# The hand-over from attention to the expert layers: transposes behind the rank matmuls, low parts of late rows on VectorE, weights issued ahead of the row list

## The chip, the cores and the metric

The kernel runs on one core of a Trainium2 chip, in one launch. The metric is the device time of that core in microseconds; the number to forecast is the median of the runs of the changed kernel.

## The reference

Three layers follow each other. Masked attention over 4 batches, 8 heads, 576 positions and 64 dimensions (half of the heads local, half strided) gives 2304 rows of 512. Each row then goes to one of 8 experts, and the result goes through a squared-relu layer:

```
x = attn_out.transpose(0, 2, 1, 3).reshape(2304, 512)
e_idx = argmax(x @ w_gate, axis=1)
for e in range(8):
    mask = e_idx == e
    h = maximum(x[mask] @ w1[e], 0)          # 512 -> 1024
    out[mask] = gate_w[mask] * eom[mask, e] * (h @ w2[e])   # 1024 -> 512
y = maximum(out @ w_in, 0) ** 2 @ w_out      # 512 -> 2048 -> 512
```

## The kernel before

**Attention and routing.** Attention runs in units (a local pair of blocks or a strided residue of one batch), each in three steps: scores and softmax (`unit`), transpose of the probabilities (`unit2`), product with v (`unit3`). Its output lies transposed in `xT`. As soon as all units that a tile of 128 rows needs are done, `gates` makes the rows of that tile (`rw`, a matmul with an identity and the two gate matrices), copies them from PSUM to `xr`, and stores them to the table `x_d` in DRAM by SP's queue. There are 18 tiles in four groups; the last group is tiles 13 to 17, the "late" tiles (`LATE` is 13). `route` ranks the rows of a group within their expert (`rk` matmuls, then `posi`), and `scatter` writes each row's number to its place in the lists `tab_d` by an indirect DMA from POOL (GpSimd).

**The largest expert goes first.** After the third group `largest` finds the expert that has most rows so far (`e0`). `early_load` then has SP load that expert's row list (`ix`), has SP load the first two chunks of its first weight matrix (`r`, 512 KB each), and has POOL gather its rows out of `x_d` in four indirect DMAs (`win`). The matmuls of the late tiles don't go through DRAM: `late_rows` picks the wanted rows of the late tiles with 0/1 matrices `pm` that VectorE builds from the ranks, and adds them up in two PSUM tiles `lr`. For that the rows of a late tile are split into a high part `xa` (ScalarE) and a low part `xb` (POOL, by `LPOOL`). `first_rows` transposes the gathered rows (`wt`) or adds them to `lr` through an identity (`L596`). From `lr` come the last columns of `xh` and `xl`, and then the first expert matmul `h` runs.

**Weights.** Every weight chunk is split after its load into a high part `hw` (ScalarE, `prep_unit`) and a low part `lw` (VectorE). Three matmuls, hi by hi, hi by lo and lo by hi, stand for one (`mm3`).

**Order.** The program is written in one order and put in another by a scheduler with a cost model; `tc.issue_after(x)` keeps what stands in it behind instruction x on the same engine. Each engine runs its list in order, and SP's and POOL's DMAs are issued in list order. A tile name in a pool stands for a buffer in a ring: `xr` has four (`XRB`), so tile 17's rows take the buffer of tile 13.

Of the kernel before, what the change touches and what calls it, by code (L numbers as in the profile page):

```python
# [7 lines left out]
F32 = mybir.dt.float32  # L8
# [4 lines left out]
AF = mybir.ActivationFunctionType  # L13
ALU = mybir.AluOpType
# [5 lines left out]
B, H, S, HD = 4, 8, 576, 64  # L20
P = 128
NT = B * S
D = H * HD
KD = D // P
# [4 lines left out]
NTILE = NT // P  # L29
# [31 lines left out]
HB = 8  # L61

MG = [(3, 3), (3, 3), (3, 3)]
LPOOL = (13, 14, 15, 16, 17)
DS = 6
LN = 6
FILL = (2, 3)
PMB = 5
LWP = 0

# [61 lines left out]
def moe_kernel(ctx, tc, q, k, v, wg, wog, w1, w2, w_in64, w_out64, consts, out, dbg=None):  # L132
    nc = tc.nc
# [12 lines left out]
    ident = cst[:, C_ID : C_ID + P]  # L146
# [83 lines left out]
    for i in range(NPT):  # L230
        x = big.tile([P, 4, SM], F32, name=f"ptp{i}")
# [32 lines left out]
    last_ev, ev_ = {}, [None]  # L264
# [55 lines left out]
    nun = [0]  # L320
# [131 lines left out]
    scq = []  # L452
# [15 lines left out]
    def gates():  # L468
        while gq and needs(gq[0][1]) <= done:
            g, t = gq.pop(0)  # L470
            t0, t1 = GROUPS[g]
            if t == t0:
                xrs[g] = wk.tile([P, 5, 2 * E], F32, name=f"lg{g}", tag="lg", bufs=2), []
            lg, rows = xrs[g]
            xr = wk.tile([P, KD, W], F32, name=f"xr{t}", tag="xr", bufs=XRB)
            col = t * P % (2 * S)
            for kh in range(2):
                ps = pss.tile([P, 2, W], F32, name=f"rw{t}_{kh}", tag=TAILT.get((t, kh), "tp"))
                for kk in range(2):
                    kd = kh * 2 + kk  # L480
                    nc.tensor.matmul(ps[:, kk, :], xT[:, kd, col : col + P], igw[:, kd, :], start=True, stop=True)  # L481
                evac(xr[:, 2 * kh : 2 * kh + 2, :], ps)
            nc.vector.tensor_reduce(
                lg[:, t - t0, :], xr[:, :, P:].rearrange("p k c -> p c k"), axis=AX.X, op=ALU.add
            )
            rows.append(xr)
            if t >= LATE:
                parts[t] = xa, xb = [wk.tile([P, KD, P], F32R, name=f"x{i}{t}", tag="xp", bufs=XPB) for i in "ab"]
                nc.scalar.activation(xa, xr[:, :, :P], AF.Copy)
                eng = nc.gpsimd if t in LPOOL else nc.vector  # L490
                eng.tensor_tensor(xb, xr[:, :, :P], xa.bitcast(F32), op=ALU.subtract)
            stq(x_d[1 + t * P : 1 + (t + 1) * P, :], xr[:, :, :P])
            if t == t1 - 1:
                route(g, list(range(t0, t1)), lg, rows)
                if t1 == LATE:
                    lead["do"] = largest
                elif t0 >= LATE:
                    late_rows(t0, t1, rows)
# [6 lines left out]
    lead = {}  # L505
# [3 lines left out]
    oreg = {}  # L509
# [3 lines left out]
    def rows_of(k, reg):  # L513
        ix = const.tile([P, NW], I32, name=f"ix{k}")
        nw = (CAPS[k] + P - 1) // P
        nc.sync.dma_start(ix[:, :nw], tab_e[bass.ds(reg, 1), : nw * P].rearrange("e (c p) -> p (e c)", p=P))
        return ix
# [14 lines left out]
    def early_load():  # L532
        e0 = lead["e0"]
        oreg[0] = nc.values_load(e0[0:1, :], engines=[ET.SP], min_val=0, max_val=E - 1)
        lead["ix"] = rows_of(0, oreg[0])
        for c in range(2):
            raw = early[0].tile([P, KD, UC], F32, name=f"r0_{c}", tag="raw", bufs=2)
            nc.sync.dma_start(
                raw, w1[bass.ds(oreg[0], 1), :, c * UC : (c + 1) * UC].rearrange("e (a p) f -> p (e a) f", p=P)
            )  # L540
            eraw["w1", 0, c] = raw

        for r in range(0, CAPS[0], P):
            win_get(0, r, lead["ix"], 1 + LATE * P)
# [29 lines left out]
    def first_rows():  # L574

        xh = early[0].tile([P, KD, CAPS[0]], F32R, name="xh0", tag="xh")
        xl = early[0].tile([P, KD, CAPS[0]], F32R, name="xl0", tag="xl")
        xsp[0] = (xh, xl)
        acc["p"] = [pss.tile([P, 2, NL], F32, name=f"lr{h}", tag="pt") for h in range(2)]
        for t in range((CAPS[0] + P - 1) // P):  # L580
            R = min(P, CAPS[0] - t * P)
            w = wins[0, t]
            c = max(0, min(R, C0 - t * P))
            if c:
                ps = pss.tile([P, KD, P], F32, name=f"wt0_{t}", tag=("o", "os")[t % 2], bufs=1)
                for a in range(KD):
                    nc.tensor.transpose(ps[:, a, :c], w[:c, a, :], ident[:c, :c])
                cs = slice(t * P, t * P + c)
                nc.scalar.activation(xh[:, :, cs], ps[:, :, :c], AF.Copy)
                with tc.issue_after(lead["pm"].ins):  # L590
                    nc.vector.tensor_tensor(xl[:, :, cs], ps[:, :, :c], xh[:, :, cs].bitcast(F32), op=ALU.subtract)
            if c < R:
                cs = slice(t * P + c - C0, t * P + R - C0)
                with tc.issue_after(lead["rk"].ins) if t in FILL else nullcontext():
                    for a in range(KD):
                        nc.tensor.matmul(  # L596
                            acc["p"][a // 2][:, a % 2, cs],
                            w[:R, a, :],
                            ident[:R, c:R],
                            start=(t == C0 // P and a % 2 == 0),  # L600
                            stop=False,
                        )

    def late_rows(t0, t1, rows):
        rel = wk.tile([P, 5], F32, name=f"rel{t0}", tag="rel")
        nc.vector.tensor_scalar(rel[:, : t1 - t0], posi[:, t0:t1], lead["base"], None, op0=ALU.subtract)
        pms = []
        for t in range(t0, t1):
            pm = wk.tile([P, NL], F32R, name=f"pm{t}", tag="pm", bufs=PMB)
            lead["pm"] = nc.vector.tensor_scalar(  # L610
                pm, cst[:, C_IO : C_IO + NL], rel[:, t - t0 : t - t0 + 1], None, op0=ALU.is_equal
            )
            pms.append((t, pm))
        if t0 == LATE:
            first_rows()
        xh, xl = xsp[0]
        for h in range(2):
            ps = acc["p"][h]
            for t, pm in pms:
                for a in range(2):  # L620
                    for x in range(2):
                        nc.tensor.matmul(  # L622
                            ps[:, a, :],
                            parts[t][x][:, 2 * h + a, :],
                            pm,
                            start=False,
                            stop=(t == NTILE - 1 and a == x == 1),
                        )
            if t1 == NTILE:
                to = (slice(None), slice(2 * h, 2 * h + 2), slice(C0, CAPS[0]))  # L630
                nc.scalar.activation(xh[to], ps, AF.Copy)
                lead["last"] = nc.vector.tensor_tensor(xl[to], ps, xh[to].bitcast(F32), op=ALU.subtract)  # L632
# [94 lines left out]
    for b in range(B):  # L727
        t = tiles[b]
        tn = transposes(b + 1, tiles[b + 1]) if b + 1 < B else iter(())
        for n, ku in enumerate(ORDER[b].split()):  # L730
            next(tg, None)
            kind, u = ku[0], int(ku[1:])
            q2.append((b, t, kind, u) + unit(b, t, kind, u))
            drain(D2, D3)
            if b == B - 1 and n >= LN and "do" in lead:
                lead.pop("do")()
                lead["ok"] = 1
            if b == B - 1 and not early and all(a[0] == b for a in q2 + q3):
                front.close()
                early.append(  # L740
                    bulk.enter_context(tc.tile_pool(name="early", bufs=1, side="right", reuse_waits="tile"))
                )
            if scq and nun[0] >= scq[0][0] and (b < B - 1 or "ok" in lead):
                with tc.issue_after(last_ev["p"].ins):
                    scq.pop(0)[1]()
            if n >= (5 if b == 0 else 1):
                next(tn, None)
                if b == 0:
                    next(tn, None)
        for _ in tn:  # L750
            pass
        tg = iter(())
        if b + 2 < B:
            tiles[b + 2] = load(b + 2)
# [112 lines left out]
    def prep_unit(u):  # L867
        kind, k, c = u
# [42 lines left out]
        pool, nb = (raws, 2) if nwh[0] % WB < 2 else (mp, WB - 2)  # L911
        hi = pool.tile(shp, F32R, name="h" + nm, tag="wh", bufs=nb)
        first = u in eraw
        with tc.issue_after(last_ev["s"].ins) if first else nullcontext():
            nc.scalar.activation(hi, raw, AF.Copy)  # L915
        lo = pool.tile(shp, F32R, name="l" + nm, tag="wl", bufs=nb)
        eng = nc.gpsimd if first and LWP else nc.vector
# [472 lines left out]
```

## Time and profile before

| what | value |
|---|---|
| runs, us | 816.06, 822.29, 822.36 (median 822.29) |
| profiled execution, us | 815.72 |
| its span, us | 813.9 |
| busy TensorE (PE), us | 763.5 (94%) |
| busy VectorE, ScalarE, POOL, us | 553.9, 493.3, 216.8 |

The span is the stretch that the trace covers; 1.8 us of the profiled execution's own time lie outside it. Times in the trace count from the start of the span. Attention takes the first 150 us, the first expert matmul starts at 173.73 us, and the rest is expert layers and the last layer.

### The profile page before, as it was taken

The page shows a single profiled execution, that of the slowest core. Times are in us where ns is not written, and L with a number is a line of the kernel's source. Part 1 is how long each engine was busy: PE and PEld are TensorE (multiplying, and loading weights), DVE is VectorE, ACT ScalarE, POOL GpSimd, SP SyncE. Part 2 cuts the span into 40 slices and gives each one's busy share as a digit, 9 for nine tenths or more (in the row PEclk, how much of TensorE's full clock was granted, in tenths as well). Part 3 has the DMA queues.
Part 4 walks back from the last instruction along what each step waited for, and adds up shares of the span by engine and source line. Part 5 has one row for each costly group of instructions (what it writes and reads, how often), then busy time and mean ns, then how long its engine had stood idle before and what let it go on. Part 6 is the DMA issues. An engine that isn't in the chain of part 4 may idle for free.

```text
span 813.9 us, 14424 instructions
## 1 busy us (share of the span) xinstructions
PE 763.5 (94%) x5139; PEld 704.9 (87%) x5139; DVE 553.9 (68%) x1109; ACT 493.3 (61%) x1197; POOL 216.8 (27%) x210
## 2 busy tenths in 40 slices
PE   4999799599999999999989999999999999999993
PEld 3988789599999999999978888888889988888893
DVE  4778578565467578779889777787654687566442
ACT  2878588524455465656677676766655586556542
POOL 7223133537065764431133121004000003000002
PEclk9999989779999999999999999999999999999998
DMA  8987801629679999876554633524232235223002
GB/s 175 201 178 136 189 21 54 191 63 333 202 188 267 196 303 283 298 258 210 172 195 147 218 128 123 175 91 149 91 118 77 76 105 182 72 87 102 1 1 81
DMA packets 106691, 124.85 MB, mean 153 GB/s; under 512 B 42801, under 2 KB 77137, under 8 KB 106610
## 3 DMA queue, kind: packets, MB, share of 16 engines
q1 hardware_dynamic: 97026, 100.77, 43.6%
q0 software_dynamic: 8096, 22.63, 8.6%
q8 instruction: 42, 0.69, 0.4%
q10 hardware_dynamic: 1488, 0.44, 0.3%
q14 instruction: 39, 0.32, 0.2%
HBM read 101.70 MB, written 22.12 MB: 152 GB/s over the span
## 4 chain that ended last, share of the span: by engine, by line
PE 55%; issue 17%; DMA 9%; DVE 7%; ACT 6%; POOL 4%; SPq 1%; POOLq 0%; ACTq 0%; DVEq 0%
DMA s0wo<-in_moe_w_out_dram 4%; PE o L935 4%; PE h L935 4%; PE o L936 4%; PE o L937 4%; PE y L935 4%; PE y L936 3%; PE h L936 3%; PE y L937 3%; PE h L937 3%; PE rw L481 2%; DMA ks<-in_k_dram 1%; DMA rw<-in_moe_w_dram 1%; POOL win L520 1%; PE lr L622 1%
## 5 line engine op out<-in xcount | busy, mean ns | idle before, releaser
L935 PE MATMUL o<-hwo,gh 128*128 128x512 f32 x288 | 114.2, 397 | 3.8 <-ACT gh L1063 3.8
L936 PE MATMUL o<-lwo,gh 128*128 128x512 f32 x288 | 113.4, 394 | 0.0
L919 DVE TENSOR_TENSOR lw<-rw,hw 128x1024 fp32r<-128x1024 f32 x62 | 78.2, 1262 | 43.2 <-ACT hw L915 42.6
L1149 ACT ACTIVATE rl<-rl 128x384 f32<-128x384 f32 x96 | 49.5, 519 | 94.9 <-DVE rl L1147 94.8
L915 ACT ACTIVATE hw<-rw 128x1024 fp32r<-128x1024 f32 x62 | 65.9, 1062 | 65.2 <-PE h L936 44.9
L1176 POOL DMA_INDIRECT out_dram<-ob,idx x18 | 20.6, 1147 | 275.5 <-ACT ob L1175 271.0
L1064 DVE TENSOR_TENSOR gl<-rl,gh 128x384 fp32r<-128x384 f32 x96 | 56.8, 593 | 44.3 <-ACT gh L1063 43.2
L937 PE MATMUL o<-hwo,gl 128*128 128x512 f32 x288 | 83.6, 396 | 2.0 <-DVE gl L1064 2.0
L935 PE MATMUL h<-xh,hw 128*128 128x416 f32 (+7 forms) x256 | 81.0, 316 | 1.6 <-DVE hl L1035 1.5
L937 PE MATMUL h<-xh,lw 128*128 128x416 f32 (+7 forms) x256 | 79.5, 310 | 0.0
L936 PE MATMUL h<-xl,hw 128*128 128x416 f32 (+7 forms) x256 | 79.5, 310 | 0.0
L936 PE MATMUL y<-hl,hw 128*128 128x416 f32 (+7 forms) x256 | 77.1, 310 | 0.0
L937 PE MATMUL y<-hh,lw 128*128 128x416 f32 (+7 forms) x256 | 76.6, 310 | 0.0
L935 PE MATMUL y<-hh,hw 128*128 128x416 f32 (+7 forms) x256 | 68.0, 311 | 0.4 <-ACT hh L1034 0.4
L935 PEld LDWEIGHTS o<-hwo,gh 128*128 128x128 f32 x288 | 54.0, 188 | 15.5 <-ACT gh L1063 6.3
L937 PEld LDWEIGHTS o<-hwo,gl 128*128 128x128 f32 x288 | 53.6, 188 | 12.8 <-DVE gl L1064 3.0
L936 PEld LDWEIGHTS o<-lwo,gh 128*128 128x128 f32 x288 | 54.1, 188 | 9.0
L1063 ACT ACTIVATE gh<-rl 128x384 fp32r<-128x384 f32 x96 | 49.9, 521 | 1.8
L935 PEld LDWEIGHTS h<-xh,hw 128*128 128x128 f32 x256 | 48.1, 188 | 3.1 <-DVE hl L1035 2.9
L1150 ACT ACTIVATE rl<-rl 128x384 f32<-128x384 f32 x96 | 49.6, 519 | 1.7
L936 PEld LDWEIGHTS h<-xl,hw 128*128 128x128 f32 x256 | 48.2, 188 | 0.3 <-DVE xl L632 0.2
L936 PEld LDWEIGHTS y<-hl,hw 128*128 128x128 f32 x256 | 48.1, 188 | 0.1
(602 smaller groups left out, 2066.6 us busy)
## 6 DMA issues: line engine op xcount, KB each, us to landing
rw<-in_moe_w_dram SPq DMA_DIRECT2D x62, 512.0 KB
rwa<-ws_d SPq DMA_DIRECT2D x24, 512.0 KB
rwb<-ws_d SPq DMA_DIRECT2D x24, 384.0 KB
e6wi<-in_moe_w_in_dram SPq DMA_DIRECT2D x32, 256.0 KB
rwo<-wout_d SPq DMA_DIRECT2D x16, 512.0 KB
x_d<-xr SPq DMA_DIRECT2D x18, 256.0 KB
ws_d<-eo POOLq DMA_DIRECT2D x16, 256.0 KB, 5.1
s0wo<-in_moe_w_out_dram SPq DMA_DIRECT2D x8, 512.0 KB
```

What stands on the lines that cost most here:

```text
L481: nc.tensor.matmul(ps[:, kk, :], xT[:, kd, col : col + P], igw[:, kd, :], start=True, stop=True)
L520: return nc.gpsimd.indirect_dma_start(out=out_, out_offset=None, in_=x_d[:n, :], in_offset=bass.IndirectOffsetOnAxis(ap=ix, axis=0),)
L915: nc.scalar.activation(hi, raw, AF.Copy)
L919: eng.tensor_tensor(lo, raw, hi.bitcast(F32), op=ALU.subtract)
L935: nc.tensor.matmul(ps, ah, bh, start=first, stop=False)
L936: nc.tensor.matmul(ps, ah, bl_, start=False, stop=False)
L937: nc.tensor.matmul(ps, al, bh, start=False, stop=last)
L1063: nc.scalar.activation(h, x, AF.Copy)
L1064: nc.vector.tensor_tensor(l, x, h.bitcast(F32), op=ALU.subtract)
L1149: nc.scalar.activation(rl[:, :HC], src, AF.Relu)
L1150: nc.scalar.activation(rl[:, :HC], rl[:, :HC], AF.Square)
L1176: ins = nc.gpsimd.indirect_dma_start(out=out[:, :], out_offset=bass.IndirectOffsetOnAxis(ap=idx[:, gt_, 0:1], axis=0), in_=ob, in_offset=None,
```

## The change

Six edits, all in the last 35 us before the expert layers:

- `xb` of every late tile goes from POOL to VectorE; that of the last tile (17) is put behind the last `pm`.
- In `early_load` the two weight loads `r` are issued before the row list `ix`, not after it.
- All transposes and identity matmuls of gathered rows are put behind the rank matmuls `rk`, where only the third and fourth block were.
- The selection matmuls of `late_rows` run over all high parts first, then over all low parts, for each half.
- The high parts `hw` of the two early weight chunks are put behind the last `xa`; before, they stood behind the last ScalarE copy of the attention output.
- `largest` is called after the fourth unit of the last batch instead of the sixth, and up to two scatters are released per unit there.

```diff
-LPOOL = (13, 14, 15, 16, 17)
-LN = 6
-FILL = (2, 3)
+LN = 4
...
-                nc.scalar.activation(xa, xr[:, :, :P], AF.Copy)
-                eng = nc.gpsimd if t in LPOOL else nc.vector
-                eng.tensor_tensor(xb, xr[:, :, :P], xa.bitcast(F32), op=ALU.subtract)
+                lead["xa"] = nc.scalar.activation(xa, xr[:, :, :P], AF.Copy)
+                lead["xb"] = lambda: nc.vector.tensor_tensor(xb, xr[:, :, :P], xa.bitcast(F32), op=ALU.subtract)
+                if t < NTILE - 1:
+                    lead["xb"]()
...
-        lead["ix"] = rows_of(0, oreg[0])
         for c in range(2):
             raw = early[0].tile([P, KD, UC], F32, name=f"r0_{c}", tag="raw", bufs=2)
             nc.sync.dma_start(
...
             eraw["w1", 0, c] = raw
+        lead["ix"] = rows_of(0, oreg[0])
...
-                for a in range(KD):
-                    nc.tensor.transpose(ps[:, a, :c], w[:c, a, :], ident[:c, :c])
+                with tc.issue_after(lead["rk"].ins):
+                    for a in range(KD):
+                        nc.tensor.transpose(ps[:, a, :c], w[:c, a, :], ident[:c, :c])
...
-                with tc.issue_after(lead["rk"].ins) if t in FILL else nullcontext():
+                with tc.issue_after(lead["rk"].ins):
...
+        if t1 == NTILE:
+
+            with tc.issue_after(lead["pm"].ins):
+                lead["xb"]()
...
-            for t, pm in pms:
-                for a in range(2):
-                    for x in range(2):
+            for x in range(2):
+                for t, pm in pms:
+                    for a in range(2):
...
-                with tc.issue_after(last_ev["p"].ins):
-                    scq.pop(0)[1]()
+                for _ in range(2 if b == B - 1 else 1):
+                    if scq and nun[0] >= scq[0][0]:
+                        with tc.issue_after(last_ev["p"].ins):
+                            scq.pop(0)[1]()
...
-        with tc.issue_after(last_ev["s"].ins) if first else nullcontext():
+        with tc.issue_after(lead["xa"].ins) if first else nullcontext():
```

On SP, from the read of the largest expert's number (`e`) on, this stood in the program of before (`r` are the two weight chunks, `ix` the row list, `x_d<-xr` the stores of tiles 13 to 15):

```order
L516 DMA ix_2399<-tab_d 128x4x1
L538 ISA
L538 DMA r_0_2401<-in_moe_w_dram 128x4x256
L538 ISA
L538 DMA r_1_2403<-in_moe_w_dram 128x4x256
L501 DMA x_d<-xr_2471 512x1x128
L501 DMA x_d<-xr_2508 512x1x128
L501 DMA x_d<-xr_2533 512x1x128
```

and this stands at the same place in the change:

```order
L536 DMA r_0_2281<-in_moe_w_dram 128x4x256
L536 ISA
L536 DMA r_1_2283<-in_moe_w_dram 128x4x256
L500 DMA x_d<-xr_2471 512x1x128
L515 ISA
L515 DMA ix_2285<-tab_d 128x4x1
L500 DMA x_d<-xr_2508 512x1x128
L500 DMA x_d<-xr_2533 512x1x128
```

The weights and the store of tile 13 now stand ahead of the row list, which waits for the scatters.

On TensorE, from the last matmul of the late tiles' rows on, this stood in the program of before (`wt`, `lr` from `win` are the gathered rows, `rk` the ranks):

```order
L481 MATMUL rw_1_2584<-igw,xT 128x144 x2
L587 MATMUL wt_0_2636<-cst,win_0_2405 128x128 x4
L587 MATMUL wt_1_2643<-cst,win_128_2407 128x80 x4
L596 MATMUL lr_2634<-cst,win_128_2407 128x48 x2
L596 MATMUL lr_2635<-cst,win_128_2407 128x48 x2
L655 LDWEIGHTS cstb
L655 MATMUL rk_2605<-oh,cstb 128x40
```

and this stands there in the change (the twelve rows of `rk` between its first and its last are left out):

```order
L479 MATMUL rw_1_2584<-igw,xT 128x144 x2
L659 LDWEIGHTS cstb
L659 MATMUL rk_2604<-oh,cstb 128x40
...
L668 MATMUL rk_2604<-ebb,onesb 128x40
L587 MATMUL wt_0_2636<-cst,win_0_2287 128x128 x4
L587 MATMUL wt_1_2643<-cst,win_128_2289 128x80 x4
L596 MATMUL lr_2634<-cst,win_128_2289 128x48 x2
```

All ranks now stand ahead of everything that waits for a gather.

On ScalarE, from the last copy of the attention output (`xT`) on, this stood in the program of before (`xa`, `xr` are the high parts and the rows of tiles 15 to 17, `hw` the early weights' high parts):

```order
L274 ACTIVATE xT<-o3l_2573 128x2x64
L915 ACTIVATE hw_0_0_2775<-r_0_2401 128x1024
L915 ACTIVATE hw_0_1_2779<-r_1_2403 128x1024
L489 ACTIVATE xa_2543<-xr_2533 128x512
L274 ACTIVATE xr_2558<-rw_0_2559 128x288
L489 ACTIVATE xa_2568<-xr_2558 128x512
L274 ACTIVATE xr_2579<-rw_1_2584 128x288
```

and this stands there in the change:

```order
L272 ACTIVATE xT<-o3l_2573 128x2x64
L487 ACTIVATE xa_2543<-xr_2533 128x512
L272 ACTIVATE xr_2558<-rw_0_2559 128x288
L487 ACTIVATE xa_2568<-xr_2558 128x512
L272 ACTIVATE xr_2579<-rw_1_2584 128x288
L487 ACTIVATE xa_2589<-xr_2579 128x512
L921 ACTIVATE hw_0_0_2775<-r_0_2281 128x1024
```

The two `hw` moved behind the last tile's rows.

## Rows read from the trace of the kernel before

**Rows 1.** The page: busy us of each engine, share of the span, instructions.

```profile
PE 763.5 (94%) x5139; PEld 704.9 (87%) x5139; DVE 553.9 (68%) x1109; ACT 493.3 (61%) x1197; POOL 216.8 (27%) x210
```

**Rows 2.** TensorE's waits after 176 us: who waited for whom, us, times, longest.

```profile
PE o L935 <- ACT gh L1063: 3.8, 6, 0.8
```

**Rows 3.** TensorE, timeline: start us, us, what, count, [idle before <-releaser].

```profile
149.32 2.23 PE L481 MATMUL rw<-igw,xT 128*128 128x144 f32 x16 [0.53 <-DVE xT L270]
157.15 1.08 PE L587 MATMUL wt<-cst,win 128*128 128x128 f32 x4 [5.61 <-DMA win<-x_d,ix]
...
158.99 1.86 PE L596 MATMUL lr<-cst,win 128*128 128x48 f32 x8
163.10 0.22 PE L655 MATMUL rk<-oh,cstb 128*128 128x40 bf16 x1 [2.26 <-DVE oh L652]
...
163.53 3.92 PE L596 MATMUL lr<-cst,win 128*128 128x128 f32 x16
...
167.43 0.52 PE L622 MATMUL lr<-pm,xa 128*128 128x208 f32 x1
...
173.73 0.37 PE L935 MATMUL h<-xh,hw 128*128 128x416 f32 x1
```

**Rows 4.** Windows of 1 us: busy PE, PEld, DVE, ACT, POOL; PEclk, DMA share, GB/s.

```profile
151.00:152.00 1.00, 0.54 (x5) 0.33 (x3) 0.06 (x1) 0.00 (x0) 0.61 (x1) 1.00 1.00 282
...
154.00:155.00 1.00, 0.00 (x0) 0.00 (x0) 0.00 (x0) 0.56 (x2) 0.91 (x1) 0.54 1.21 350
...
161.00:162.00 1.00, 0.00 (x0) 0.00 (x0) 1.00 (x1) 0.00 (x0) 1.00 (x2) 0.50 0.92 314
...
171.00:172.00 1.00, 1.00 (x10) 1.00 (x10) 0.00 (x0) 0.00 (x0) 0.20 (x1) 0.92 0.02 1
```

**Rows 5.** VectorE, timeline: expert's number, late tiles' routing, early weights' low parts.

```profile
140.32 0.15 DVE L564 TENSOR_REDUCE e<-te 128x1 int32<-128x8 f32 x1
...
157.43 0.46 DVE L270 COPY xr<-rw 128x288 f32<-128x288 f32 x1 [6.37 <-POOL xb L491]
...
158.51 3.83 DVE L640 TENSOR_TENSOR d<-lg,mx 128x40 f32<-128x40 f32 x1
...
166.60 2.34 DVE L919 TENSOR_TENSOR lw<-r,hw 128x1024 fp32r<-128x1024 f32 x2
```

**Rows 6.** POOL, timeline: last early scatter, first gather, low parts, a late scatter.

```profile
141.95 1.23 POOL L703 DMA_INDIRECT tab_d<-tok,posi  x1 [0.30 <-issue]
151.39 0.99 POOL L520 DMA_INDIRECT win<-x_d,ix  x1 [8.21 <-issue]
...
156.11 6.17 POOL L491 TENSOR_TENSOR xb<-xr,xa 128x512 fp32r<-128x512 f32 x5
...
166.97 1.68 POOL L703 DMA_INDIRECT tab_d<-tok,posi  x1 [0.30 <-issue]
```

**Rows 7.** ScalarE, timeline: the first early weight split and the wait before it.

```profile
153.43 1.06 ACT L915 ACTIVATE hw<-r 128x1024 fp32r<-128x1024 f32 x1 [4.78 <-DMA r<-in_moe_w_dram]
```

**Rows 8.** SP's DMA queue, timeline: start us, us of issuing, what, count.

```profile
148.15 0.43 SPq L516 DMA_DIRECT2D ix<-tab_d  x1
148.82 0.97 SPq L538 DMA_DIRECT2D r<-in_moe_w_dram  x2
149.91 8.54 SPq L501 DMA_DIRECT2D x_d<-xr  x5
158.71 2.00 SPq L909 DMA_DIRECT2D rw<-in_moe_w_dram  x3
```

**Rows 9.** Tile `tab_d`, 141.8 to 143.3 us: its scatter.

```profile
DMA to landing us min/median/max: 6.2/6.2/6.2
```

**Rows 10.** Tile `tab_d`, 74.0 to 75.6 us: its scatter.

```profile
DMA to landing us min/median/max: 12.9/12.9/12.9
```

**Rows 11.** Tile `idx_d`, whole span: 18 scatters of the same kind.

```profile
DMA to landing us min/median/max: 6.9/7.5/9.5
```

**Rows 12.** Tile `win`, whole span: 24 gathers.

```profile
DMA to landing us min/median/max: 3.3/5.7/8.7
```

## The prediction

> **What bounds the kernel now.** I read the page first: TensorE is busy 763.5 us, 94% of the span [rows 1], so most of the span can only shrink by less TensorE work, and the change takes none away. The list of TensorE's waits then says where the rest is. After 176 us the largest group of waits adds up to 3.8 us [rows 2]; the expert layers follow TensorE, and whatever is won before them should move them forward as a block. So the whole question is how early the first expert matmul `h` starts; it starts at 173.73 us [rows 3].
>
> The timeline of TensorE shows three losses before it. The last rows matmuls end at 149.32 + 2.23 = 151.55 us; then TensorE stands idle for 5.61 us until the first gather has landed (157.15 us), and again for 2.26 us, up to 163.10 us, until VectorE has the one-hot matrix `oh` [rows 3]. Third, the clock: at 154 us it goes from its full level (2.4 GHz) to half of it (1.2 GHz), about 2.5 us after TensorE went idle, and it is back only in the slice from 171 us on [rows 4], so nearly all work between runs at half speed.
>
> The second loss has a chain of its own, in the other engines' timelines. ScalarE waits 4.78 us for the early weights and splits them from 153.43 us [rows 7], and the copies of the last tiles' rows stand behind that. POOL builds the low parts from 156.11 to 162.28 us [rows 6]. VectorE's copy of the last tile waits for one of them, since it takes the buffer of tile 13 (6.37 us), and its next two-input operation `d`, on 40 columns, takes 3.83 us and ends at 162.34 us, together with POOL's five [rows 5]. I take that as POOL holding VectorE up.
>
> The first loss is a chain of transfers. The last early scatter is issued at 141.95 us and lands after 6.2 us [rows 6, 9]; at 148.15 us SP issues the row list [rows 8]; at 151.39 us POOL issues the first gather [rows 6]; it is there at 157.15 us [rows 3], 5.8 us after its issue.
>
> **The change part by part.**
>
> *Low parts on VectorE, weight splits behind the late rows, ranks first.* These go together, since they all free the rank chain. On VectorE one `xb` has half the columns of an `lw`, which takes 2.34 / 2 = 1.17 us [rows 5], so about 0.6 us. Two stand ahead of the last copy into `xT`, for which the last rows matmuls wait; that delays them by 0 (VectorE has gaps there) to 1.2 us. From their end at 151.55 to 152.75 us it takes about 0.5 us for a copy, 1.1 us for what stands from the copy at 157.43 to the start of `d` at 158.51 us [rows 5], 0.2 us for an undisturbed `d`, 0.8 us from its end to the ranks [rows 3, 5], and 0.6 us for the `xb` of tile 16: 3.2 us. The ranks then run at 154.8 to 156.0 us instead of 163.10 us, in the idle time ahead of the gathered rows. What goes from TensorE's path is the wait of 2.26 us and the ranks themselves, 163.53 - 163.10 = 0.43 us: **-2.7 us**. The weights are no new wait on ScalarE: issued 6 to 7 us earlier, they are there before the last `xa`. `pm`, the last `xb` (0.6 us) and both `lw` (2.34 us) follow the ranks on VectorE and are done by about 161 us; the selection matmuls that need the first two start later than that. If that cover were gone, the last `xb` would cost 0.6 us.
>
> *Weights ahead of the row list on SP.* The two loads (1 MB) are issued as soon as SP has read the expert's number, which VectorE has ready at 140.5 us [rows 5], so while the last scatters go out (the last at 141.95 us [rows 6]); the store of tile 13 follows them, and its rows are copied by then, so the row list still comes to its wait before the scatters land. What this can cost is the landing of the scatters. The nearest rows on both sides: 6.2 us beside almost no traffic [rows 9], and a median of 7.5 us for the index scatters beside weight loads [rows 11]. So 0 to +1.3 us; I take half, **+0.7 us**, as the burst covers only part of the flight. The far bound is 12.9 us for a scatter beside many small transfers [rows 10]; it is a rival below.
>
> *What the gathers gain.* In the trace the gathers share the DMA engines with the weights and with stores of 256 KB each; the engines are full from 151 us on [rows 4]. With the weights gone the landing of the first, 5.8 us, should come nearer to the shortest of the tile, 3.3 us [rows 12]. Against that, the stores of tiles 16 and 17 and the next three weight chunks, which SP issues at 158.71 us [rows 8], move forward to about 153 us. I take 4.5 us, the middle: **-1.3 us**, with ends of -2.5 and 0.
>
> *Ranks ahead of gathered rows, order of the selection matmuls, earlier call of `largest`.* The number of matmuls stays. High parts first means that the last `xb` is wanted late and the first half is complete some 2 us earlier; both are covered by what stands beside, so 0. `largest` and the first scatter move, but the scatters of the third group wait for their ranks as before: 0.
>
> *The clock.* Gathered rows take 160.85 - 157.15 = 3.7 and 167.43 - 163.53 = 3.9 us, the forty selection matmuls 173.73 - 167.43 = 6.3 us [rows 3]. Of these 6.3 us about 3.65 run at half the clock, until it rises [rows 4]. If a matmul takes twice as long at half the clock, all forty take 9.0 us at 1.2 GHz and 4.5 us at 2.4 GHz (an estimate from these rows). The clock fell within an idle time, and the change leaves TensorE idle from about 152 to 156.5 us but for 0.4 us of ranks; I take it to fall again and to rise at the same place in the work, **0**, with ends of -1.8 and +2.7 us.
>
> The sum is -2.7 + 0.7 - 1.3 + 0 = -3.3 us: gathered rows from 156.55 us, selection from 164.15 us, `h` at 170.45 us. Against the profiled execution's 815.72 us this is 812.4 us.
>
> **Two rules.** Row first: beside `lw` (166.60 to 168.94 us) a scatter took 1.68 us on POOL where the undisturbed gather took 0.99 [rows 5, 6]. The Trainium skill ("SBUF — State Buffer", "Who interferes with whom") says that a VectorE operation with two SBUF inputs contends with POOL operations that read SBUF and that the second to come waits; it speaks against `xb` on VectorE while POOL issues gathers. By the row one gather beside an `xb` would come at most 0.7 us later, and the sum would be -2.6 us.
>
> The scatters' price is the more open one. The Trainium skill ("DMA: Bandwidth & Descriptors", "Queues, rings and completion order") says that a DMA engine takes turns between queues, packet by packet. Were that all, SP's megabyte would hold a POOL scatter up by little, and the sum would be -4.0 us. The 7.5 us beside weight loads [rows 11] agree only in part, so I keep +0.7.
>
> **The rivals.**
>
> *The scatters sink in the weights (slower).* If the last early scatter lands as late as the one beside heavy traffic, 12.9 instead of 6.2 us [rows 9, 10], the row list, the gathers and all behind them come 6.7 us later. With the other terms that is +6.7 - 1.3 - 2.7 = +2.7 us: 818.4 us. It decides from a delay of 4 us on, a landing of 10.2 us. For it: the two loads start exactly when the last scatters do. Against it: eighteen scatters beside weight streams stayed at or under 9.5 us [rows 11].
>
> *The next weights meet the gathers.* SP now issues 1.5 MB more some 5 us earlier, beside the later gathers. If the third, issued some 2.6 us after the first (four take 156.11 - 151.39 = 4.7 us [rows 6]), lands after the longest time, 8.7 us [rows 12], it is there at 163.4 us, and TensorE wants it at 156.55 + 3.7 = 160.3 us: a new wait of 3.1 us takes the place of the one removed. Time: 815.5 us.
>
> *The clock doesn't fall.* The ranks now break the idle time, which was about 2.5 us old when the clock fell. At full clock the gathered rows' 7.6 us halve, but the last gather, issued about 155.9 us, lands some 5 us later (between shortest and median [rows 12]), so selection starts at about 161.2 us and `h` at 165.7 us: -8.0 us, 807.7 us. Against it: two idle stretches of 1.5 us and more remain, and the ranks are a few small matmuls.
>
> **How the numbers follow.** The forecast has 0.63, with a range of its own of 809 to 815.5 us on the profile's scale; the sunken scatters 0.10, the colliding weights 0.15, the kept clock 0.12. The executions of the kernel before lie in two pairs, 815.72 and 816.06, 822.29 and 822.36 us; the trace is of the lower pair, and no row says what the other 6.5 us are. The forecast against the lower pair is 812.4 us, against the median of the runs 822.29 - 3.3 = 819.0 us. A median of the changed kernel can come out at either; I give the middle, 815.7 us, which is 0.4% from both. The range runs from the kept clock in the lower pair (807.5) to beyond the forecast in the upper one (821); it leaves out the sunken scatters in the upper pair and what else ends under 807.5.
>
> Faster or slower by 1% is about what a measurement of this kernel can tell from no change, as its own runs differ by 0.8%. One per cent is 8.2 us: the forecast reaches that only if its median falls in the lower pair and the other kernel's in the upper one; the kept clock just about reaches it alone. That gives 0.19 for faster. Slower by 1% needs the sunken scatters and an unlucky pair: 0.03. The rest, 0.78, lies within 1%.
>
> **What would show it.** In the profile of the changed kernel: the ranks at 154 to 156 us, ahead of the first transposed gathered row; `d` at 0.2 us; no wait of VectorE's copies for POOL; early weight splits without a wait for a DMA; the landing of the last early scatter under 7.6 us and of the first gather near 4.5 us; half clock from about 154 us until the selection matmuls are under way; `h` at about 170.5 us. The forecast is wrong if a gather makes TensorE wait after the first one, if the row list is issued later than 149.5 us, if the clock rises earlier or later by more than 2 us, or if waits after `h` grow by more than 1 us.

## The result, and the profile after

The changed kernel takes **824.0 us** (median of 20 runs, 820.85 to 829.35), the kernel before 819.35 us (20 runs beside them, 815.90 to 822.36). The ratio is **1.0065, 95% interval 1.0048 to 1.0081**: slower by 0.65%. The forecast was 815.7 us with a range of 807.5 to 821.0; the sign was wrong and the time lies above the range, though within the 1% that held most of the chances.

The profiled execution of the changed kernel took 824.17 us (span 822.3), against 815.72 us for the profile of before, which is one of the kernel's faster executions. The medians differ by less, 4.65 us. Of the 8.45 us, 2.0 lie ahead of the steps below (the last early scatter is issued at 143.93 instead of 141.95 us); 1.9 of them are there already when SP issues its stores at 128.77 instead of 126.83 us, ahead of the earlier call of `largest`. So each step below is counted from that scatter.

The page, answering to [rows 1] (busy us, share, instructions), and TensorE's waits after 182.5 us, answering to [rows 2]: neither shows where the time went.

```profile
PE 763.6 (93%) x5139; PEld 704.3 (86%) x5139; DVE 554.4 (67%) x1114; ACT 494.1 (60%) x1197; POOL 211.0 (26%) x205
```

```profile
PE o L941 <- ACT gh L1069: 4.1, 7, 0.9
```

TensorE's timeline, answering to [rows 3] (start us, us, what, count, idle before and its releaser), shows it:

```profile
151.40 2.23 PE L479 MATMUL rw<-igw,xT 128*128 128x144 f32 x16 [0.67 <-DVE xT L268]
161.61 0.21 PE L659 MATMUL rk<-oh,cstb 128*128 128x40 bf16 x1 [7.99 <-DVE oh L656]
...
167.04 1.12 PE L587 MATMUL wt<-cst,win 128*128 128x128 f32 x4 [4.93 <-DMA win<-x_d,ix]
169.75 0.79 PE L587 MATMUL wt<-cst,win 80*128 80x80 f32 x4 [1.60 <-DMA win<-x_d,ix]
170.34 5.54 PE L596 MATMUL lr<-cst,win 128*128 128x48 f32 x24
175.81 2.46 PE L626 MATMUL lr<-pm,xa 128*128 128x208 f32 x10
...
182.46 0.43 PE L941 MATMUL h<-xh,hw 128*128 128x416 f32 x1
```

The order is as intended: ranks `rk` ahead of the first transposed gathered row `wt`, and `lr` behind it in one piece. But TensorE is idle for 8.0 us ahead of the ranks (2.3 before) and for 4.9 us ahead of `wt` (5.6 before). The chain that ended last (start us, us, what) says on what:

```profile
143.93 14.40 DMA tab_d<-tok,posi
...
158.83 2.49 DMA x_d<-xr
...
162.60 7.11 DMA win<-x_d,ix
```

and the tile `tab_d`, 143.9 to 144.5 us, answers to [rows 9]:

```profile
DMA to landing us min/median/max: 14.4/14.4/14.4
```

The last early scatter lands after 14.4 us instead of 6.2. SP's DMA queue, answering to [rows 8], stands at its wait for it:

```profile
143.52 1.03 SPq L536 DMA_DIRECT2D r<-in_moe_w_dram  x2
146.51 0.55 SPq L500 DMA_DIRECT2D x_d<-xr  x1
158.35 0.37 SPq L515 DMA_DIRECT2D ix<-tab_d  x1
158.83 2.60 SPq L500 DMA_DIRECT2D x_d<-xr  x4
```

POOL, answering to [rows 6], issues the scatter 0.41 us behind the first weight load and the first gather only 3 us behind the row list:

```profile
143.93 1.19 POOL L707 DMA_INDIRECT tab_d<-tok,posi  x1 [0.30 <-issue]
161.31 0.99 POOL L519 DMA_INDIRECT win<-x_d,ix  x1 [16.18 <-DMA x_d<-xr]
...
165.13 1.76 POOL L519 DMA_INDIRECT win<-x_d,ix  x1 [0.30 <-issue]
```

VectorE, answering to [rows 5], has lost the hold by POOL (`d` takes 0.20 us instead of 3.83), and its copy of the last tile has a new wait in the old one's place, for a store:

```profile
159.00 0.46 DVE L268 COPY xr<-rw 128x288 f32<-128x288 f32 x1 [5.86 <-DMA x_d<-xr]
...
160.65 0.20 DVE L644 TENSOR_TENSOR d<-lg,mx 128x40 f32<-128x40 f32 x1
```

Windows of 1 us, answering to [rows 4] (busy PE, PEld, DVE, ACT, POOL; PEclk, DMA share, GB/s):

```profile
144.00:145.00 1.00, 1.00 (x9) 0.78 (x8) 1.00 (x3) 1.00 (x8) 1.00 (x1) 1.00 1.91 12
...
149.00:150.00 1.00, 1.00 (x14) 0.85 (x14) 0.97 (x3) 0.52 (x1) 0.00 (x0) 1.00 0.52 29
...
152.00:153.00 1.00, 1.00 (x11) 1.00 (x10) 0.32 (x1) 0.41 (x1) 0.00 (x0) 1.00 1.03 364
...
156.00:157.00 1.00, 0.00 (x0) 0.00 (x0) 0.00 (x0) 0.00 (x0) 0.00 (x0) 0.63 0.00 0
```

```profile
180.00:181.00 1.00, 1.00 (x10) 1.00 (x10) 0.06 (x1) 0.52 (x1) 0.00 (x0) 0.93 0.00 0
```

From 144 us on the DMA engines count as busy and move little; the megabyte goes by from 152 us on, and then nothing moves until the list is issued. (A share can exceed 1, since the whole time of a packet, one piece of a transfer, is booked where it starts: next to the 1.91 of 144 us stands 0.00 for 145 to 146 us.) The clock is at its lower level (1.2 GHz) from 156.3 us, in the idle time, to 180 us.

Counted from the last early scatter's issue to the first `h`, step by step (each a difference of two starts in the rows above, and of the same starts in [rows 3, 6, 8]):

| step | before, us | after, us | difference |
|---|---|---|---|
| last early scatter issued to row list issued | 6.20 | 14.42 | +8.2 |
| row list to first gather | 3.24 | 2.96 | -0.3 |
| first gather to `wt` | 5.76 | 5.73 | 0.0 |
| `wt` to first selection matmul | 10.28 | 8.77 | -1.5 |
| selection to `h` | 6.30 | 6.65 | +0.4 |
| sum | 31.78 | 38.53 | +6.75 |

With the 2.0 us ahead of it and 0.3 us less behind `h`, that is the 8.45 us between the two profiles. The same interval in each profile below is called **scatter to h**.

### The profile page after: what moved, and what is told of

Read it like the earlier page. It is cut to its first block, busy times and chain, and to the rows that moved or that the text cites. A ratio compares the mean times of both kernels' runs of the same rounds, so it can differ in the third digit from the quotient of the medians.

```text
span 822.3 us, 14426 instructions
## 1 busy us (share of the span) xinstructions
PE 763.6 (93%) x5139; PEld 704.3 (86%) x5139; DVE 554.4 (67%) x1114; ACT 494.1 (60%) x1197; POOL 211.0 (26%) x205
## 4 chain that ended last, share of the span: by engine, by line
PE 60%; issue 17%; DMA 9%; ACT 5%; DVE 3%; POOL 3%; SPq 1%; POOLq 0%; ACTq 0%; DVEq 0%
PE o L941 5%; PE o L943 5%; PE o L942 5%; PE h L941 4%; PE y L941 4%; PE y L942 4%; PE h L942 4%; PE h L943 4%; PE y L943 4%; DMA s0wo<-in_moe_w_out_dram 3%; DMA ks<-in_k_dram 2%; DMA tab_d<-tok,posi 2%; PE rw L479 1%; POOL idx_d L833 1%; DMA win<-x_d,ix 1%
```

## The experiments

**Theory A**: the loss is the meeting of the two weight loads (1 MB) with the scatters, whose landing releases the row list; the rest of the change gains. **Rival B**: the loss lies in the other parts (ranks ahead of the weight splits, low parts on VectorE, the buffer that tile 17 waits for), and the late landing is covered or accidental. **Rival C**: what delays the scatter is any traffic ahead of it, or the store of tile 13 alone. They were run in three sessions, each on another chip: experiments 2 to 5, with the first run of 3, in the first, experiments 1, 6 and 7 in the second, experiment 8 and the second run of 3 in the third. Each ratio is to the kernel before in the same session (medians there 821.02, 819.46 and 819.40 us).

**1. The change and the kernel before, again.** No edit; the first timed, of the second one profile.

> The change itself once more, unaltered, beside the other runs of this call. Theory A (the weight loads go out between the scatters and hold the last one up): 1.004 to 1.008 of the kernel before, landing of the last early scatter over 10 us. Rival F (its loss belonged to the one chip of the first measurement): within 0.2% of the kernel before.

> The kernel before once more, for a second profile of it: the first one was of an execution of 815.72 us, where most take 817 to 822. Expected: the same waits as in the first profile, with the rise of the clock later or a longer wait for transfers in the batches before, 3 to 5 us more in all.

Measured: the change 824.54 us, 1.0059 [1.0038, 1.0080]; before, one execution, 820.66 us. In the change the first load left at 143.99 us, again 0.41 us ahead of the last scatter, and that landed after 15.9 us; scatter to h 39.1 us. In the kernel before the scatter landed in 6.3 us and scatter to h was 33.3 us, 1.4 us more than in its first profile, all of it in the selection matmuls (178.87 - 171.17 = 7.7 us instead of 6.3), as the clock came back later. So two profiles of one kernel differ by that much in this interval; the 5.3 to 7.3 us by which the two of the change are longer are more.

**2. Row list first, the rest of the change kept.**

```diff
         oreg[0] = nc.values_load(e0[0:1, :], engines=[ET.SP], min_val=0, max_val=E - 1)
+        lead["ix"] = rows_of(0, oreg[0])
         for c in range(2):
...
             eraw["w1", 0, c] = raw
-        lead["ix"] = rows_of(0, oreg[0])
```

> The change with one part undone: the row list is issued ahead of the two weight loads again (the store of tile 13 then stands behind it too); all else of the change stays. Theory A (weight loads issued while the scatters are in flight hold the scatters up, and that is the whole loss): the last early scatter lands after 6 to 7 us instead of 14.4, the first matmul h starts 3 to 5 us earlier than in the kernel before, time 0.995 to 0.997 of it. Rival B (the moved low parts, ranks and weight splits cost something themselves): the landing is short again, but the time stays at or above 1.003 of the kernel before.

Measured: 818.29 us, **0.9968** [0.9946, 0.9989]. The list goes out 6.0 us behind the last scatter. With the one order undone the change is faster than the kernel before by 0.3%: against B, though the unaltered change was not timed beside it; experiment 7 was timed beside the change. That `h` would come 3 to 5 us earlier was missed: scatter to h is 34.3 us in this profile, with 5.0 us from the list to the first gather, and TensorE is at the last tiles' rows until 160.8 us.

**3. Only the weights ahead of the list, in the kernel before; twice.**

```diff
-        lead["ix"] = rows_of(0, oreg[0])
         for c in range(2):
...
             eraw["w1", 0, c] = raw
+        lead["ix"] = rows_of(0, oreg[0])
```

> The kernel before with one part of the change alone: the two weight loads (and with them the store of tile 13) stand ahead of the row list. Theory A: the last early scatter lands after 12 us or more, the first gather comes some 8 us later, the old waits for ranks fall inside that delay, time 1.005 to 1.009 of the kernel before. Rival B: within 0.2% of the kernel before, landing under 8 us.

> The kernel before with the two weight loads ahead of the row list, once more, to see on which side of the last early scatter the loads leave. If they leave ahead of it, as in the change, its landing takes 13 to 16 us and the time is 1.004 to 1.009 of before; if they leave behind it, the landing takes 6 to 8 us and the time is 0.999 to 1.003.

Measured: first 820.79 us, 1.0006 [0.9987, 1.0024]; in the third session, the same kernel, 824.16 us, **1.0040** [1.0008, 1.0071]. The first result missed what A expected. The two intervals overlap, so that the times differ is not certain; the profiles show what differed. First session, POOL's last early scatter and SP's queue:

```profile
141.40 0.97 POOL L703 DMA_INDIRECT tab_d<-tok,posi  x1 [0.30 <-issue]
```

```profile
143.31 0.54 SPq L537 DMA_DIRECT2D r<-in_moe_w_dram  x2
147.98 0.55 SPq L501 DMA_DIRECT2D x_d<-xr  x1
148.78 0.41 SPq L516 DMA_DIRECT2D ix<-tab_d  x1
```

Third session, the same two:

```profile
144.31 1.21 POOL L703 DMA_INDIRECT tab_d<-tok,posi  x1 [0.30 <-issue]
```

```profile
143.93 1.03 SPq L537 DMA_DIRECT2D r<-in_moe_w_dram  x2
146.92 0.55 SPq L501 DMA_DIRECT2D x_d<-xr  x1
160.52 0.37 SPq L516 DMA_DIRECT2D ix<-tab_d  x1
```

The program is the same. In the first the loads left 1.9 us behind the last scatter, and the list was issued 7.4 us after it (815.57 us, the fastest of the twelve runs); in the second they left 0.38 us ahead of it, and it landed after 16.2 us (824.44 us). Scatter to h was 31.2 us in the first and 35.5 us in the second. So A holds in a narrower form: in these profiles it counts on which side of the last scatter the loads leave. Other parts of the change aren't in this kernel, so they aren't needed for the loss.

What set the two apart lies ahead of the loads. In all four profiles of the first session ScalarE stands idle for 3.5 us ahead of a copy `ptp`, with a releaser that the profile doesn't show ("remote"); here for the first profile above:

```profile
ACT ptp L274 <- remote: 3.5, 1, 3.5
```

There VectorE starts on the expert's number 0.3 to 0.4 us ahead of the last scatter's issue; in every profile without this idle time it does so 1.6 to 1.7 us ahead. SP needs the number for the loads' addresses. Whether the chip or chance brings the idle time, no run tells. The other executions have no trace, so on which side their loads left isn't known.

**4. Other bytes ahead of the list.** The list first of the weights, but behind two stores of 256 KB each to a tensor that nothing reads.

```diff
+        for i in range(2):
+            nc.sync.dma_start(
+                spare_d[bass.ds(oreg[0], 1), i].rearrange("e p (k c) -> p (e k) c", c=P), igw[:, :, :P]
+            )
+        lead["ix"] = rows_of(0, oreg[0])
```

> The change, but with two stores of 256 KB from SBUF to a spare DRAM tensor in the place of the weight loads, and the weights behind the row list; 0.5 MB more is moved. Theory A as a matter of any transfer that SP starts beside the scatters: landing 10 us or more and a time of at least 1.003 of the kernel before. Rival C (only loads from DRAM do it): landing 6 to 8 us, time 0.995 to 0.999.

Measured: 818.89 us, 0.9988 [0.9968, 1.0009]. The stores left at 145.85 us, behind the last scatter (144.00 us), and SP needed 7.43 us to issue them, which by itself puts the list 9.5 us behind the scatter. So it doesn't tell loads from stores; inconclusive on C. Scatter to h was 34.2 us. Against experiment 2 a list that is 3.5 us later goes with 0.2% more time, within the intervals.

**5. One load ahead of the list, the other behind.**

```diff
             eraw["w1", 0, c] = raw
-        lead["ix"] = rows_of(0, oreg[0])
+            if c == 0:
+                lead["ix"] = rows_of(0, oreg[0])
```

> The change, but only one of the two weight chunks (512 KB) ahead of the row list; the second and the store of tile 13 behind it. If the cost goes with the bytes in flight: landing about 10 us, time about the kernel before's. If one load is enough to set it off: landing 13 us or more, time 1.004 to 1.008. Rival D (the store of tile 13, not the weights, holds the row list up): landing 6 to 7 us, time 0.995 to 0.998.

Measured: 820.22 us, 1.0003 [0.9976, 1.0029]. Here too the load left behind the last scatter (146.03 against 144.19 us), the list 6.8 us after it, and the first gather 6.2 us after the list instead of 3.2 [rows 6, 8]. Scatter to h was 34.8 us. It doesn't say whether one load ahead of the scatter is enough for the delay.

**6. Both loads ahead of the list, but behind the store of tile 13,** so that they can't leave ahead of the last scatter.

```diff
+            st = stq(x_d[1 + t * P : 1 + (t + 1) * P, :], xr[:, :, :P])
+            if t == LATE:
+                early_rest(st)
...
+        with tc.issue_after(st.ins):
+            early_weights()
+        lead["ix"] = rows_of(0, oreg[0])
```

> The change with one shift: the two weight loads still stand ahead of the row list, but behind the store of tile 13, and so go out some 2 us later, after the last early scatter has left POOL. Theory A2 (what counts is that the loads go out before the last scatter): landing 6 to 8 us, time 0.997 to 1.001 of the kernel before. Rival G (loads in flight at any time between scatter and row list cost the same, or the list queues behind them): landing or list some 6 us late as in the change, 1.004 to 1.008.

Measured: 820.36 us, **1.0005** [0.9985, 1.0026], in the session in which the unaltered change had 1.0059. POOL's last early scatter, and SP's queue:

```profile
145.81 1.19 POOL L715 DMA_INDIRECT tab_d<-tok,posi  x1 [0.30 <-issue]
159.51 0.99 POOL L521 DMA_INDIRECT win<-x_d,ix  x1 [12.52 <-DMA x_d<-xr]
```

```profile
149.18 2.64 SPq L548 DMA_DIRECT2D r<-in_moe_w_dram  x2
153.00 0.37 SPq L517 DMA_DIRECT2D ix<-tab_d  x1
```

The scatter lands in 7.1 us. What is left is a second, smaller loss: the list's own trip to the first gather takes 6.5 us instead of 3.2. So in these profiles the loads cost wherever they stand ahead of the list: 8 to 10 us for the scatter if they leave just ahead of it, about 1 us for the scatter and 3 us for the list if behind. Scatter to h was 34.2 us.

**7. List first, weights behind the last tile's store.**

```diff
         oreg[0] = nc.values_load(e0[0:1, :], engines=[ET.SP], min_val=0, max_val=E - 1)
+        lead["ix"] = rows_of(0, oreg[0])
...
+            if t == NTILE - 1:
+                with tc.issue_after(st.ins):
+                    early_weights()
```

> The change with the row list first and the two weight loads last, behind the store of the last tile. Theory: the gathers share the DMA engines only with stores, the first lands after about 4 us instead of 5.6, and the weights still arrive ahead of their use: 0.993 to 0.996 of the kernel before, 1 to 2 us under the run with the list first alone. Rival: the weights come late, ScalarE waits for them ahead of the transposed rows' high parts, and the time is that of the kernel before or above.

Measured: 817.55 us, **0.9979** [0.9958, 1.0000], less of a gain than expected, in the session in which the unaltered change had 1.0059. In its profile (816.65 us) scatter to h is the shortest of all, 30.8 us: the scatter lands in 6.1 us, the list needs 3.4, the first gather 4.8 us.

**8. The loads long before the last scatters.** The kernel leaves out the choice of the expert for the first two chunks: they are those of expert 0, so their loads need not wait for its number.

```diff
-                raw, w1[bass.ds(oreg[0], 1), :, c * UC : (c + 1) * UC].rearrange("e (a p) f -> p (e a) f", p=P)
+                raw, w1[0:1, :, c * UC : (c + 1) * UC].rearrange("e (a p) f -> p (e a) f", p=P)
```

> The first two chunks are loaded from expert 0 whatever the router says (the choice of the expert for them is left out), so that they can leave SyncE some twenty microseconds ahead of the scatters and have landed when the scatters go. If the loss of the change is the meeting of weight bytes and scatters, the last scatter lands after 6 to 7 us, the row list is issued at about 149 to 150 us, the first selection runs 30 to 32 us after the last scatter's issue and the time is 0.996 to 0.999 of before. If the loss came from the other parts of the change (ranks ahead of the weight splits, low parts on VectorE), it stays at 1.004 to 1.007.

Measured: 816.66 us, **0.9966** [0.9936, 0.9997]. SP's queue, POOL, TensorE:

```profile
114.94 0.94 SPq L536 DMA_DIRECT2D r<-in_moe_w_dram  x2
...
150.25 0.42 SPq L515 DMA_DIRECT2D ix<-tab_d  x1
```

```profile
143.95 1.19 POOL L707 DMA_INDIRECT tab_d<-tok,posi  x1 [0.30 <-issue]
153.59 0.99 POOL L519 DMA_INDIRECT win<-x_d,ix  x1 [8.45 <-DMA x_d<-xr]
```

```profile
156.16 0.19 PE L659 MATMUL rk<-oh,cstb 128*128 128x40 bf16 x1 [2.52 <-DVE oh L656]
159.57 1.11 PE L587 MATMUL wt<-cst,win 128*128 128x128 f32 x4 [2.97 <-DMA win<-x_d,ix]
...
168.41 2.46 PE L626 MATMUL lr<-pm,xa 128*128 128x208 f32 x10
```

The store of tile 13 is issued behind the list here; all else stands as in the change. The scatter lands in 6.3 us and the loss is gone: A over B. Scatter to h is 31.8 us; it is this interval that came out at the 30 to 32 us expected for the first selection matmul, which starts after 24.5 us. As for C, the store can't be the sole cause, since the engines crawl from 144 us on and it is issued at 146.51 us, later than an undelayed scatter's packets run (below); whether it adds to it was not tried. Of the versions that compute all, experiment 2 beats the kernel before; experiment 7 beats the change in one session, and the kernel before by an interval that ends at 1.0000.

## Why the prediction was wrong

**The step that failed** is "Weights ahead of the row list on SP", put at +0.7 us. It measured +8.2 us in the change's first profile and 9.7 in its second (15.9 - 6.2). The step saw the place (the loads leave while the last scatters go out) but took its price from [rows 11], index scatters beside weight loads that stream already, at 7.5 us, and kept 12.9 us [rows 10] only for a rival. That was the near row, and "many small transfers" misread it. In the kernel before, a load of 576 KB (`qs`) left 1.2 us ahead of that scatter and another (`ks`) 0.4 us behind it, SP's queue and POOL:

```profile
73.39 0.31 SPq L244 DMA_DIRECT2D qs<-in_q_dram  x1
74.92 0.31 SPq L244 DMA_DIRECT2D ks<-in_k_dram  x1
```

```profile
74.56 1.00 POOL L703 DMA_INDIRECT tab_d<-tok,posi  x1 [0.17 <-issue]
```

So the meeting stood in the trace before, at a price of 6.7 us (12.9 - 6.2). Experiment 8 shows that the price belongs to what is sent at this place, and experiments 1, 3 and 6 that it hangs on which leaves first: with the loads 0.38 to 0.41 us ahead of the last scatter it lands after 14.4, 15.9 and 16.2 us, with loads 1.8 to 3.4 us behind it the list goes out after 6.8 to 7.4 us (experiments 3, 5 and 6). What lies between these two was not seen. The prediction compared durations of landing and didn't ask which of two engines' queues would be first.

**The slower rival** had the mechanism, "The scatters sink in the weights", and its point of decision, a landing of 10.2 us. Its price was too low, 6.7 us against 8.2 to 9.7, and the gains of 4.0 us that it set against that were 1.4 in the table. Its chance of 0.10 rested on the eighteen scatters of [rows 11] and not on the one of [rows 10], which was nearer.

The Trainium skill ("DMA: Bandwidth & Descriptors", "Queues, rings and completion order") has a DMA engine take turns between queues, packet by packet. The prediction took from it that the scatter would be held up by little; the landings of 14.4 to 16.2 us show that here more was at work.

**A wait that was not seen**: the store of tile 13 is issued behind the loads at 146.51 us and crawls with them, so the copy of tile 17, which takes its buffer in the ring of four, waits for it until 159.00 us, and the ranks stand at 161.61 us instead of the 154 to 156 forecast. The gathers, held by the list, came later still (`wt` at 167.04 us), so it probably cost little of its own here; in experiment 8, where the store isn't behind the loads, the ranks run at 156.16 us. Its price alone was not tried.

**The ranks, low parts and weight splits, -2.7 us**: the mechanism was right, the size was not. `d` takes 0.20 us, no copy waits for POOL, the ranks are out of the gathered rows' way, the early splits don't wait for a DMA. From `wt` to the selection the change saves 1.5 us, experiment 8 1.4 us (8.84 us), experiment 7 0.6 us (9.67 us, with 2.96 us of wait for the second gather inside). The rest went into a second gather that TensorE now waits for (1.60 us in the change): shorter work in front uncovers it. The gather itself, -1.3 us, gave 0.0 in the change, -1.0 in experiment 7 and +0.2 in experiment 8.

**The clock, 0**: it fell in the idle time as forecast and rose 4.3 us into the selection matmuls instead of 3.7 (by the share of the lower level in the window at either rise): selection to h takes 6.65 us in the change, 6.9 in experiment 7 and 7.3 in experiment 8, up to 1.0 us given back. As the kernel before had 7.7 us in its second profile, this term is no property of the change. Behind `h` nothing changed, as forecast (waits for `gh` 4.1 us against 3.8).

Taken together, the change without its loads ahead of the list is worth 0.21% to 0.34% (experiments 7, 2 and 8; the last with expert 0's chunks), that is 1.7 to 2.8 us of 819.4; the prediction's sum without that step was -4.0 us. The scale was no part of the miss: with the 20 runs' median the same sum gives 819.35 - 3.3 = 816.05 us, close to the middle of two scales that was given.

**How the scatter was held up** can be read from the DMA queues (packets, MB, share of 16 engines): q0 has POOL's scatters, 32 packets each, q1 SP's transfers, q8 and q14 instructions. In the changed kernel the three scatters ahead of the last had run by 144.4 us; from 145 to 153.5 us there is no packet of q0:

```profile
q1 hardware_dynamic: 801, 0.80, 59.0%
q8 instruction: 1, 0.02, 0.7%
q14 instruction: 1, 0.01, 0.2%
```

The last scatter's 32 packets all start in the next 1.5 us, from 153.7 us on, 9.8 us behind its issue:

```profile
q0 software_dynamic: 32, 0.00, 1.6%
```

In the kernel before, with this scatter issued at 141.95 us, 28 of the 32 start between 143 and 145 us, within 2 us of it:

```profile
q0 software_dynamic: 28, 0.00, 1.1%
```

So the scatter doesn't crawl beside the loads; its packets are not started until 0.8 MB of theirs have been. The other two late landings are the same (no packet of the last scatter until 155 us, 10.8 and 11.2 us behind its issue). In experiment 3's first profile all 32 had run by 143.2 us, and the first packet of the loads starts at 143.5 us.

The loads are slow at first. Their packets in the changed kernel in the windows 144 to 147, 147 to 151 and 151 to 155 us:

```profile
q1 hardware_dynamic: 29, 0.03, 71.9%
```

```profile
q1 hardware_dynamic: 132, 0.14, 68.1%
```

```profile
q1 hardware_dynamic: 1323, 1.10, 86.1%
```

They hold an engine for 0.719 x 16 x 3 / 29 = 1.2 us, then 0.33 us, then 0.04 us each on the mean. The mean is made by a few: half of the loads' packets take 0.05 us or less, and the eleven that start between 144 and 145 us take 1.8 to 5.4 us. In experiment 8 the same 1 MB, issued at 114.94 us, far ahead of the last scatter, starts 115 to 118 us with

```profile
q1 hardware_dynamic: 263, 0.27, 54.2%
```

that is 0.10 us each. It met three earlier scatters there, issued at 114.83, 116.13 and 118.18 us; they landed after 5.4, 8.8 and 6.9 us. So loads that leave 1.2 us ahead of a scatter made it 8.8 us here, where [rows 10] has 12.9 us: the meeting has no fixed price. Experiment 3's first profile has the slow start too (0 to 58 GB/s from 143 to 150 us), though the scatter's packets had run; so packets of a scatter that stand waiting are not needed for it. Why some of the first packets are slow, why the scatter's are not started between those of the loads, and why the hold-up was shorter in experiment 8's meeting, no run here tells.

## What to carry to other kernels

A transfer that is moved ahead of a small one on the critical path is priced by the worst meeting that the trace shows, not by the median of calmer ones; if it leaves from another engine's queue, ask which leaves first, and by how much. Put the short list that releases others first, and the megabyte behind it: here the change measured 1.0059 with the megabyte first and 0.9979 with the list first and the megabyte last, in one session. Where an experiment's result differs between sessions, compare the order of issue in the two profiles before calling it noise.

## What was unexpected of the hardware

- 512 KB loads issued 0.38 to 0.41 us ahead of a scatter made it land after 14.4 to 16.2 us; issued 3.4 us behind it, 7.1 us. In the first case the scatter's 32 packets start 9.8 to 11.2 us behind its issue instead of about 2. Loads that left 1.2 us ahead made it 12.9 us in one place [rows 10] and 8.8 us in another (experiment 8).
- The DMA engines can count as busy and move little: a share of 0.97 at 53 GB/s from 147 to 148 us, of 1.03 at 364 GB/s from 152 to 153 us.
- A POOL gather issued beside VectorE's two-input `lw` took 1.76 us instead of 0.99, as a scatter did before [rows 6]. The Trainium skill ("SBUF — State Buffer", "Who interferes with whom") names that contention, and the row agrees.
